# Loading k one third of a block before its use, and attention heads 1.15 slots apart

## The chip, the cores and the metric

The kernel runs on one core of a Trainium2 chip. The metric is device time in microseconds (us), the median over several runs of the whole program. One further execution was recorded by the profiler. Its engines are called PE (TensorE), DVE (VectorE), ACT (ScalarE), POOL (GpSimd) and SP (SyncE, which here only issues transfers).

## What is computed

Two things follow each other, for 8 batches of 576 tokens. First comes attention with 8 heads of width 64, in which every 8 rows of k and of v are averaged, so that a head has 72 keys. Then comes a block of two residual mixes: over tokens with `w_tok`, and over channels with two matrices and a ReLU between them. Cut down, the reference is:

```
k_p = k.reshape(B, H, 72, 8, D).mean(axis=3)       # B, H, S, D = 8, 8, 576, 64
v_p = v.reshape(B, H, 72, 8, D).mean(axis=3)
attn = softmax(q @ k_p^T / sqrt(D))
x = (attn @ v_p), heads side by side               # (B, 576, 512)
tok = einsum('ts,bsd->btd', w_tok, alpha1 * x + beta1)
u = x + lam * tok
ch = relu((alpha2 * u + beta2) @ w_ch1) @ w_ch2    # 512 -> 2048 -> 512
out = u + lam * ch
```

Everything comes in and goes out as float32; the matrix products run on 16-bit operands.

## The kernel before, in words

**Chunks and blocks.** The tokens of a batch are split into four chunks of 128 (c = 0 to 3) and a rest of 64. The rests of two neighbouring batches share one more chunk (c = 4). That gives 36 chunks, and four consecutive ones form a block of 512 columns for the channel mix, so there are nine blocks, n = 0 to 8. The loop over n at the end of the kernel makes, for each block, a list `todo` of (slot, action), sorts it by slot and emits it. The order on every engine and on every queue is therefore written out by these slot numbers; each engine then runs its own list in order, and waits only for data and buffers.

**The channel mix sets the slots.** In block n, `mlp_A(n, j)` stands at slot j, for j = 0 to 15: four matmuls (L477) into a PSUM tile `ps_h`, which ACT turns into `Hj` (L482). `mlp_B(n, m, part)` stands at slot 16 + 4m + part: four matmuls (L495) of output chunk m. Its last part adds the result to `u_sb` on DVE (L500) and stores it from SP's queue (L502, or L506 for a shared chunk).

**Attention of the next batch runs in between.** Block n, for n up to 6, also holds `attention(b)` for b = n + 1:

- `cast_rem` (L116, L118) and `sum_k` (L131, L133) on POOL take the sums of k's rows, and the cast of q's last 64 rows, from the tiles `k_raw` and `rem_raw`. They stand at the block's very start (slots -2.0 to 0.3). POOL has little else to do and runs ahead of the other engines: it begins them as soon as the loads have landed, which can be in the block before.
- `att_F` (L314) and `att_Frem` (L332) are DMA transposes of q on SP's queue, at the block's start. Head 0 needs them at slot 7.4.
- `att_V` (L362, L364) sums v's rows on DVE, and `att_K` brings k's sums through PE and copies them to `kpT` (L356, DVE).
- Head h has `att_S` at slot 7.4 + 1.0 h (PE L374 and L377 into `ps_sc`, exponential on ACT L379), and `att_AV` two slots later (PE L393 and L397 into `ps_av`; on DVE the reciprocal L399 and `x_tm` L401). After every second head `att_X` multiplies `x_tm` by a row into `xs` (DVE L408 and L412).
- `mix_T(b, c)` from slot 18.6 is the token mix: five matmuls into `ps_tok` (L442), then `u_sb` (L444) and `u_bf` (L446) on DVE. `mix_uT` 1.8 slots later is a DMA transpose of `u_bf` into `u_fm` (L456, SP's queue), which `mlp_A` of a later block reads.

The tiles `ps_h`, `ps_sc`, `ps_av` and `ps_tok` share six PSUM buffers (pool `psA`), so that PE can't start the next `ps_h` while DVE has not read an older `ps_av`.

**Loads.** In block n the loads of batch b + 1 = n + 2 are issued. Before the change k and the rests (`load_qk` and `load_rem`: on SP's queue two `k_raw` loads L88 and four `rem_raw` loads L96) stand at slots 0.4 to 1.6. `load_qk` also issues q's load, L79, from POOL's queue, where it comes behind the sums of batch b. v (`load_v`, L108, SP's queue) is at 3.5 and 7.5. `k_raw`, `rem_raw` and `v_u` have two buffers each, `q_bf` has four. Batch 1, which is set up during block 0, and the loads of batch 2 there have slots of their own (the branches `late` and `b == 1`).

## Time and profile before

| | |
|---|---|
| median of 7 runs | 381.56 us (380.48 to 383.31) |
| the profiled execution | 381.88 us, of which 380.1 us is the span from first to last instruction |
| granted PE clock | 0.995 of full speed |
| busy in the span: PE, DVE, ACT, POOL | 350.0, 237.3, 157.2, 85.2 us |
| block 1 begins at | 87.49 us |
| blocks 2 to 5 begin at | 126.35, 165.39, 204.08, 242.87 us |
| blocks 6 to 8 begin at | 282.86, 319.92, 347.55 us |

A block begins where its first `ps_h` matmul starts in the chain of waits. The page gives each engine's busy time, the span in 40 slices, the chain of work that ended last, and groups of equal instructions. The trace behind it can be asked for any stretch of time: what each engine did in it, what it waited for, and how busy the core's 16 DMA engines were. "Busy" of PE counts overlapping matmuls once, and is not PE at its peak.

### The profile page before, as it was taken

How to read it: one execution, taken by the hardware profiler on the slowest of the kernel's cores; microseconds unless marked ns; L12 is line 12 of the kernel's file. 1: busy time of each engine (PE TensorE's matmuls, PEld its weight loads, DVE VectorE, ACT ScalarE, POOL GpSimd, SP SyncE). 2: the span in 40 equal slices, each digit the busy share in tenths (PEclk: the TensorE clock that was granted, in tenths of full speed). 3: DMA queues.
4: the chain of work that ended last, by engine and by line, in shares of the span. 5: the costliest groups of instructions: out<-in, count | busy, mean ns of one | idle time of the engine just before them, and what ended most of it. 6: DMA issues, size and time to landing. Idle time of an engine off the chain costs nothing.

```text
span 380.1 us, 5735 instructions
## 1 busy us (share of the span) xinstructions
PE 350.0 (92%) x2139; PEld 188.8 (50%) x2179; DVE 237.3 (62%) x459; ACT 157.2 (41%) x317; POOL 85.2 (22%) x94
## 2 busy tenths in 40 slices
PE   2889999699989989999999999997999999999994
PEld 0475655345644554455445544464446544544541
DVE  4796839888885588658864887489647872011011
ACT  1574667116910483038303830284018602712700
POOL 7563353930530062005300430024000000000000
PEclk9999999989999999999999999999999999999999
DMA  8999996745953495468635872775233024002011
GB/s 199 226 178 214 262 212 173 120 83 153 243 82 100 120 236 82 98 145 217 102 96 126 212 116 64 131 202 112 56 106 68 0 57 124 0 29 83 2 55 55
DMA packets 63931, 46.93 MB, mean 123 GB/s; under 512 B 31448, under 2 KB 54044, under 8 KB 63904
## 3 DMA queue, kind: packets, MB, share of 16 engines
q1 hardware_dynamic: 54496, 38.55, 41.4%
q0 software_dynamic: 9408, 8.02, 13.9%
q8 instruction: 17, 0.28, 0.3%
q14 instruction: 10, 0.08, 0.1%
HBM read 38.04 MB, written 9.44 MB: 125 GB/s over the span
## 4 chain that ended last, share of the span: by engine, by line
PE 80%; DVE 12%; DMA 2%; issue 1%; ACT 1%; SPq 1%; POOL 1%; POOLq 0%; DVEq 0%
PE ps_ch L495 32%; PE ps_h L477 28%; PE ps_tok L442 11%; DVE xs L408 3%; DVE x_tm L401 3%; PE ps_sc L374 3%; DVE xs L412 3%; DMA vecs<-in_moe_beta_dram 2%; PE ps_av L393 1%; SPq L314 1%; DVE rec L399 1%; PE ps_sc L377 1%; DMA rem_qT<-rem_q 1%; PE ps_uT L461 1%; PE ps_w L247 1%
## 5 line engine op out<-in xcount | busy, mean ns | idle before, releaser
L482 ACT ACTIVATE Hj<-ps_h,bias_cols 128x512 bf16<-128x512 f32 x144 | 98.5, 687 | 164.3 <-PE ps_h L477 162.9
L477 PE MATMUL ps_h<-u_fm,w 128*128 128x512 bf16 (+2 forms) x572 | 136.0, 375 | 9.0 <-DVE x_tm L401 8.1
L495 PE MATMUL ps_ch<-w,Hj 128*128 128x512 bf16 x562 | 133.3, 381 | 0.7
L477 PEld LDWEIGHTS <-w 128*128 128x128 bf16 x592 | 62.7, 114 | 55.6 <-DVE x_tm L401 10.4
L495 PEld LDWEIGHTS <-Hj 128*128 128x128 bf16 x576 | 55.4, 98 | 63.5 <-issue 0.8
L500 DVE TENSOR_TENSOR u_sb<-u_sb,ps_ch 128x512 f32<-128x512 f32 x36 | 24.6, 685 | 78.4 <-PE ps_ch L495 78.3
L442 PE MATMUL ps_tok<-xs,wtT 128*128 128x512 bf16 (+1 forms) x195 | 50.4, 386 | 3.3 <-DVE xs L408 2.7
L379 ACT ACTIVATE ET<-ps_sc 72x256 f16<-72x256 f32 (+1 forms) x128 | 44.3, 401 | 5.0 <-PE ps_sc L374 4.2
L444 DVE TENSOR_TENSOR u_sb<-x_tm,ps_tok 128x512 f32<-128x512 f32 (+1 forms) x40 | 27.5, 687 | 29.9 <-PE ps_tok L442 29.6
L362 DVE TENSOR_TENSOR v_u<-v_u 72x512 f32<-72x512 f32 x64 | 38.4, 600 | 1.5
L116 POOL CAST rem_q<-rem_raw 128x256 bf16<-128x256 f32 x7 | 2.8, 395 | 141.2 <-DMA rem_raw<-in_q_dram 141.2
L442 PEld LDWEIGHTS <-wtT 128*128 128x128 bf16 (+1 forms) x200 | 19.5, 99 | 27.2 <-issue 5.4
L401 DVE TENSOR_TENSOR x_tm<-ps_av,rec 128x320 f32<-128x320 f32 x64 | 31.5, 492 | 2.3
L408 DVE TENSOR_TENSOR xs<-x_tm,lamal_bc 128x512 bf16<-128x512 f32 x29 | 28.5, 982 | 0.9
L374 PE MATMUL ps_sc<-qT,kpT 128*72 128x256 bf16 x128 | 26.6, 291 | 1.7 <-ACT kpT L356 1.3
L446 DVE TENSOR_TENSOR u_bf<-u_sb,al_bc 128x512 bf16<-128x512 f32 (+1 forms) x38 | 27.1, 713 | 1.5
L393 PEld LDWEIGHTS <-ET 72*128 72x128 f16 x256 | 16.6, 102 | 13.4 <-issue 0.8
L133 POOL TENSOR_TENSOR k_bf<-k_raw 128x512 bf16<-128x512 f32 x16 | 22.8, 1425 | 1.3
L131 POOL TENSOR_TENSOR k_raw<-k_raw 128x512 f32<-128x512 f32 x16 | 21.5, 1346 | 3.8 <-DMA k_raw<-in_k_dram 3.8
L393 PE MATMUL ps_av<-vp,ET 72*128 72x66 f16 x256 | 18.5, 199 | 0.6 <-ACT ET L379 0.4
L356 DVE CAST kpT<-ps_kp 64x288 bf16<-64x288 f32 x28 | 12.7, 455 | 7.1 <-PE ps_kp L351 6.5
L399 DVE RECIPROCAL rec<-ps_av 128x5 f32<-128x5 f32 x64 | 12.1, 189 | 8.0 <-PE ps_av L397 6.9
(98 smaller groups left out, 214.8 us busy)
## 6 DMA issues: line engine op xcount, KB each, us to landing
k_raw<-in_k_dram SPq DMA_DIRECT2D x16, 512.0 KB
v_u<-in_v_dram SPq DMA_DIRECT2D x16, 512.0 KB
out_dram<-u_sb SPq DMA_DIRECT2D x32, 256.0 KB
w<-in_moe_w_ch_dram POOLq DMA_DIRECT2D x8, 512.0 KB, 12.5
q_bf<-in_q_dram POOLq DMA_DIRECT2D x12, 256.0 KB, 4.8
q_raw<-in_q_dram SPq DMA_DIRECT2D x4, 512.0 KB
rem_raw<-in_q_dram SPq DMA_DIRECT2D x16, 64.0 KB
rem_raw<-in_k_dram SPq DMA_DIRECT2D x16, 64.0 KB
```

The source lines that it names most:

```text
L362: nc.vector.tensor_tensor(out=t[:, :, 0:n], in0=t[:, :, 0:n], in1=t[:, :, n:2 * n], op=ALU.add)
L374: nc.tensor.matmul(out=ps_sc[0:SPG, 0:256], lhsT=kpT_pool[u][:, half, h % 4, :], rhs=st["qT"][u][:, 2 * (h % 4):2 * (h % 4) + 2, :])
L379: nc.scalar.activation(out=ET[:, n0:n0 + n], in_=ps_sc[0:SPG, 0:n], func=AF.Exp, bias=0.0, scale=0.125)
L393: nc.tensor.matmul(out=av[:, c, :], lhsT=ET[:, m0:m0 + 128], rhs=vp1[:, hh, :])
L401: nc.vector.tensor_tensor(out=x[:, :, dd:dd + D], in0=av[:, :, 0:64], in1=rec.unsqueeze(2).to_broadcast((P, 5, D)), op=ALU.mult)
L408: eng.tensor_tensor(out=xs[:, 0:4, cols], in0=x[:, 0:4, cols], in1=lamal_bc[:, cols].unsqueeze(1).to_broadcast((P, 4, D * (h1 - h0))), op= ...
L442: nc.tensor.matmul(out=ps_tok, lhsT=wtT[0:kk, at, t0:t0 + P], rhs=xs[0:kk, sc, :], start=(sc == 0), stop=(sc == 4))
L444: nc.vector.tensor_tensor(out=s["u"][p0:p1, :], in0=st1[b]["x"][p0:p1, c, :], in1=ps_tok[p0:p1, 0:DM], op=ALU.add)
L446: eng.tensor_tensor(out=s["u_bf"][p0:p1, :], in0=s["u"][p0:p1, :], in1=al2_bc[p0:p1, :], op=ALU.mult)
L477: nc.tensor.matmul(out=ps_h[:, t0:t1], lhsT=w1_of(cc, j), rhs=u_fm[n][:, cc, t0:t1], start=(cc == 0), stop=(cc == 3))
L482: nc.scalar.activation(out=t, in_=ps_h, func=AF.Relu, bias=bias_cols[:, j:j + 1], scale=1.0)
L495: nc.tensor.matmul(out=ps, lhsT=Hj[n, j][:, 128 * m:128 * m + 128], rhs=w2[j // 4][:, j % 4, :], start=(j == 0), stop=(j == NJ - 1))
```

## The change

Three slot numbers move.

- For all batches but the first ones, k's and the rests' loads of batch b + 1 move within block n from slots 0.4 to 1.6 to slots 21.0 to 21.2, that is from the block's first instructions to a place behind the first `mix_uT`. v's loads stay. On POOL's queue the order of instructions does not change at all; only the data that its sums wait for are asked for later.
- `att_S`, and with it `att_AV` and `att_X`, of head h moves from 7.4 + 1.0 h to 7.4 + 1.15 h, again for all batches but the first ones.
- `mix_T` of chunk c, and `mix_uT` behind it, moves from 18.6 + 1.3 c to 19.1 + 1.3 c.

```diff
@@ attention(b)
         for h in range(8):
-            at = 17.0 + 0.9 * h if late else 7.4 + 1.0 * h
+            at = 17.0 + 0.9 * h if late else 7.4 + 1.15 * h
             lag = 1.6 if late else 2.0
             todo.append((at, lambda h=h: att_S(b, h)))
@@
         for c in range(5):
-            at = 26.2 + 0.9 * c if late else 18.6 + 1.3 * c
+            at = 26.2 + 0.9 * c if late else 19.1 + 1.3 * c
             todo.append((at, lambda c=c: mix_T(b, c)))
@@ the loop over n
                 for u in range(2):
-                    at = 20.0 + 0.2 * u if b == 1 else 0.4 + 1.2 * u
+                    at = 20.0 + 0.2 * u if b == 1 else 21.0 + 0.2 * u
                     todo.append((at, lambda b=b, u=u: load_qk(b + 1, u)))
                     at = 22.0 + 0.2 * u if b == 1 else 3.5 + 4.0 * u
                     todo.append((at, lambda b=b, u=u: load_v(b + 1, u)))
-                todo.append((20.1 if b == 1 else 0.9, lambda b=b: load_rem(b + 1)))
+                todo.append((20.1 if b == 1 else 21.1, lambda b=b: load_rem(b + 1)))
```

The order of instructions that results, in a block with attention: on SP's queue the two `k_raw` and four `rem_raw` loads go from behind `att_Frem` to between the block's first and second `u_fm` transposes. On PE heads 4 to 7 each come one group of four matmuls later than before, and so do the token mixes of chunks 0, 1, 3 and 4. On DVE the first L500 of the block comes ahead of the first L444 instead of behind it, and the second L500 stands ahead of the fourth L444. On POOL nothing moves.

## The prediction

> **What bounds the kernel now.** I began with the page's chain of work that ended last. PE carries most of it, and DVE is the only other engine with a large share:

> ```profile
> PE 80%; DVE 12%; DMA 2%; issue 1%; ACT 1%; SPq 1%; POOL 1%; POOLq 0%; DVEq 0%
> ```

> DVE's 12% is 46 us, so the next question is where a block loses PE time. I cut each attention block at its first `ps_tok` matmul (L442) and asked for the busy time by stage: from the block's start to the first mix, and from there to the next block. Columns: stretch, its length, then busy us of PE, PEld, DVE, ACT and POOL with counts, granted clock, DMA share, GB/s.

> ```profile
> 87.49:109.71 22.22, 20.59 (x150) 12.15 (x152) 19.07 (x41) 16.07 (x33) 8.53 (x8) 1.00 0.75 175
> 126.35:148.77 22.42, 20.62 (x150) 12.16 (x152) 19.39 (x41) 15.49 (x32) 7.97 (x8) 1.00 0.80 174
> ...
> 242.87:266.22 23.35, 20.75 (x150) 12.16 (x152) 20.05 (x41) 15.60 (x32) 6.88 (x6) 1.00 0.70 147
> 282.86:303.26 20.40, 20.24 (x150) 12.23 (x152) 17.09 (x41) 15.49 (x32) 0.00 (x0) 1.00 0.19 43
> ...
> 148.77:165.39 16.62, 16.57 (x77) 7.57 (x77) 8.78 (x14) 0.00 (x0) 0.00 (x0) 1.00 0.36 88
> 303.26:319.92 16.66, 16.61 (x78) 7.56 (x77) 8.86 (x14) 0.00 (x0) 0.00 (x0) 1.00 0.36 87
> ```

> All stages of a kind have the same matmuls. The mix stage takes 16.6 us in every block, all of it PE, while DVE is busy for half of it and POOL idle. The attention stage takes 22.05 to 23.35 us in blocks 1 to 5 (blocks 3 and 4: 22.05 and 22.13), but 20.40 us in block 6. Block 6 is the one where POOL does nothing, since no batch is left to load: an experiment that the kernel makes by itself. DVE has 2.3 us less there on the same 41 instructions. The timelines of DVE, block 2 and then block 6, show which:

> ```profile
> 138.20 1.20 DVE L408 TENSOR_TENSOR xs<-x_tm,lamal_bc 128x512 bf16<-128x512 f32 x1
> 139.42 1.26 DVE L412 TENSOR_TENSOR xs<-x_tm,lamal_bc 64x128 bf16<-64x128 f32 x1
> ...
> 294.71 0.69 DVE L408 TENSOR_TENSOR xs<-x_tm,lamal_bc 128x512 bf16<-128x512 f32 x1
> 295.41 0.29 DVE L412 TENSOR_TENSOR xs<-x_tm,lamal_bc 64x128 bf16<-64x128 f32 x1
> ```

> The slow ones are those that run while POOL sums (136.31 to 143.09 in block 2). DVE then reads `ps_av` late, the PSUM buffer comes free late, and PE waits in its timeline:

> ```profile
> 141.49 1.05 PE L477 MATMUL ps_h<-u_fm,w 128*128 128x512 bf16 x4 [1.14 <-DVE x_tm L401]
> ```

> So the bound is PE, except in attention stages of blocks 1 to 5, where DVE slowed by POOL's sums holds it up.

> [...] L408 and L412 (two SBUF inputs) go from 0.69 and 0.29 us up to 1.75 and 1.35, while L401 (one input in PSUM) keeps 0.49 us beside the same sums. [...] The trace before shows no stretch where q's load (POOL's queue) runs beside the q transposes (SP's queue), so that price is open; I bound it below.

> **The change part by part.**

> *The sums leave the attention stage.* In block 6's order of PE work the first mix will start one group of four L495 (0.86 us) later, at 21.26 us after the block's start, plus 1.08 for the mix and 1.4 for L444 and L446; the first `u_fm` transpose is issued at about 23.8. Behind it SP issues k and the rests at 25.1 to 28.8 (k 0.53, four times 0.62, k 0.54). Before, the sums' first instruction started 4.6 to 6.3 us after the first k issue (131.66 to 136.31; 92.69 to 98.94) and the sums took 6.6 to 7.3 us. So they run from about 29.8 to 36.5 of a block of 37.06 (20.40 + 16.66), in the mix stage. There DVE has only L446 of chunks 3 and 4 with two SBUF inputs, 0.69 us each, and is idle for 8 of 16.6 us; no PE work of that stage waits for `u_bf`. The gain, if the stage falls to block 6's: (22.22 + 22.42 + 22.05 + 22.13 + 23.35) - 5 x 20.40 = **10.17 us**. I take off 0.3 for spill of the sums into the next block's L362 (two SBUF inputs).

> *Sums too late?* `att_K` uses `k_bf` at 4.3 us of the next block, 4.9 us after 36.5. Covered.

> *SP's queue.* The 3.7 us of issues now stand ahead of the second `u_fm` transpose and everything behind it. The second goes out at 28.9 instead of about 25, the second store next, and the third, the last one that the very next block can need (blocks 2 and 3), at 30.6. Before, it went out later than that: SP stood at the store of the block's second output until 119.57, and the third transpose was issued at 120.42, 32.9 us into block 1. A transpose landed 2.3 us after its issue in the one case that the chain shows (`rem_qT`); with some 1.5 us of k's last packets ahead the third lands at 34.4 of 37. Cost nothing, cover 2.6 us. The head of the block loses the same 3.7 us from SP, so v's loads go out earlier; nothing waits for them.

> *What is late next: q's load.* POOL's order is unchanged, so q of batch b + 2 is issued right behind the sums of b + 1. Before, that was after 106.21, in the middle of a block, with no other transfer. Now it is at 36.5, its packets from about 38.3 (1.8 us later, as 220.54 to 222.3), which is 1.2 us into blocks 2 to 5: right on the q transposes. The stages of one us (same columns), first q's load, then transposes in block 6:

> ```profile
> 109.00:110.00 1.00, 1.00 (x7) 0.41 (x5) 0.66 (x2) 0.00 (x0) 0.00 (x0) 1.00 1.40 181
> 286.00:287.00 1.00, 1.00 (x6) 0.48 (x5) 0.30 (x2) 0.82 (x2) 0.00 (x0) 1.00 0.93 176
> ```

> Both fill the DMA engines: q's two loads for 3.4 us (shares 0.09, 1.05, 1.40, 1.36, 0.26 from 107 on), the three transposes for 3.0 us (0.56, 1.00, 0.93, 1.01, 0.33 from 284 on, some 0.8 of it a store). Alone the transposes land at about 5.5 us of a block (288.3), and L377 wants the last, `rem_qT`, at 7.3 (290.17). Together they need 1.2 + 3.4 + 3.0 = 7.6. There is no slack to hide more: in block 5 they came last already, by the chain of waits:

> ```profile
> 248.06 2.31 DMA rem_qT<-rem_q
> ```

> It landed at 250.4, 7.5 us into block 5, with no q load beside it. The wait added per block is bounded by 0 (the load's packets leave gaps that the transposes fill) and by 1.9 (half of q's 3.4 us on top of block 5's 7.5, less 7.3); the sum of the two works says 0.3. I take **0.8 us, in four blocks: 3.2 us** back.

> *Heads 1.15 apart, mixes half a slot later.* Block 6 runs at 1.0 with PE busy 20.24 of 20.40, so spacing has nothing left to give once POOL is away. A head then costs PE 1.45 us (1.15 x 0.86 + 0.46) against DVE's 1.32. Between the last `att_AV` and the first mix stand two L495 groups (1.73 us) as before; DVE needs 1.5 us to L408. Zero; bounds -0.3 and +0.3 per block if DVE still trails. L500 ahead of the first L444 costs 0.69 us on `u_bf`, with slack of over 2 us.

> **Sum.** Profiled execution 381.88 (span 380.1 and 1.78 around it); - 10.17 + 0.3 + 3.2 = 375.2. The median before, 381.56, lies 0.3 under the profiled run, so I predict **375.0**.

> **Rivals.**
> - *A, as worked out* (0.52): 373 to 378.
> - *B, the transposes fit in* (0.20): no stall, 381.6 - 10.2 = 371.4. For it: the DMA share of q's load goes to 1.4, so packets overlap, and the sums may end early.
> - *C, the interference moves* (0.12): the sums run 2 us late, into L362 and `kpT`, and slow DVE ahead of head 0; half the gain stays, 377 to 380. Against: POOL itself ran in 6.6 us beside a busier DVE.
> - *D, `u_fm` late* (0.07): k's packets hold the third transpose for over 3 us; up to 3 us in blocks 2 and 3 besides A, about 381, no change.
> - *E, q's load starves the transposes* (0.09): slower. [...] PE stands at L377 for 3 us in four blocks, and that with C's loss of 1 to 2 in each makes 383. It decides from 2.5 us per block (10.17 / 4).

> The change doing nothing is excluded: POOL's sums wait for loads that are issued 20 slots later.

> **How the numbers follow.** The range reaches from B's end (371.2) to the weak ends of A and C (379.5: 371.4 + 0.3 + four stalls of 1.9). A measurement of this kernel can tell 0.3%, 1.1 us, from no change. Faster: A, B, C = 0.84; same: D = 0.07; slower: E = 0.09.

> **What would show it.** Right: L408 at 0.69 us in blocks 1 to 5, POOL's sums in the last 8 us of each block, no PE wait on `x_tm`, attention stages near 21.3 us to the mix in block 1 and 0.5 to 1.5 longer in 2 to 5, with `rem_qT` last in the chain at L377. Wrong: L446, L362 or L356 stretched, `ps_h` waiting for `u_fm` at a block's start, or L377 held for over 2 us.

## The result: 1.4% slower, and the profile after

The changed kernel takes 386.91 us (median of 12 runs, 384.57 to 390.17) against 382.12 us before (31 runs). The ratio is 1.0141, with a 95% interval of 1.0115 to 1.0167. The profiled execution has a span of 384.5 us, 4.4 more than before, at a granted clock of 0.981 instead of 0.995.

The page's chain that ended last has exchanged DVE for DMA:

```profile
PE 83%; DVE 7%; DMA 5%; issue 2%; POOL 1%; SPq 0%; ACT 0%; POOLq 0%; DVEq 0%
```

The same cut by stage as before, at the first `ps_tok` matmul of each block, shows where. Columns: stretch, length, then busy us of PE, PEld, DVE, ACT and POOL with counts, granted clock, DMA share, GB/s. The first three lines are the attention stages of blocks 1, 2 and 5, the last is the mix stage of block 1.

```profile
85.50:106.76 21.26, 21.11 (x154) 12.66 (x156) 16.82 (x42) 15.96 (x33) 0.00 (x0) 1.00 0.47 109
122.54:146.15 23.61, 21.43 (x154) 12.59 (x156) 17.10 (x41) 15.71 (x32) 1.36 (x2) 1.00 0.64 109
...
244.06:271.44 27.38, 24.06 (x154) 13.42 (x156) 16.77 (x41) 15.82 (x32) 1.35 (x2) 0.88 0.57 98
...
106.76:122.54 15.78, 15.67 (x72) 7.16 (x73) 9.75 (x13) 0.00 (x0) 6.92 (x7) 1.00 0.65 168
```

POOL's sums have moved: 6.92 us of them lie in the mix stage, which is no longer for it. DVE is back at 17 us in the attention stage. Block 1 takes 21.26 us, which is block 6's 20.40 plus the one group of 0.86 us that now comes ahead of the mix. Blocks 3 and 4, not shown, take 25.50 and 24.85 us. So blocks 2 to 5 lie 2.35, 4.24, 3.59 and 6.12 us over block 1, 16.3 us in sum; that eats the 10.2 us won and more. PE's timeline in block 3 shows how such a block is lost:

```profile
170.90 0.38 PE L374 MATMUL ps_sc<-qT,kpT 128*72 128x256 bf16 x2 [1.69 <-DMA qT<-q_bf]
172.03 0.24 PE L377 MATMUL ps_sc<-rem_qT,kpT 128*72 128x64 bf16 x1 [0.75 <-DMA rem_qT<-rem_q]
172.11 1.88 PE L477 MATMUL ps_h<-u_fm,w 128*128 128x512 bf16 x4
```

Head 0 waits for q's transposes, first for `qT`, then for `rem_qT`. (In blocks 2 and 5 the view puts the first of the two waits down to DVE's L362, which only ended last. L374 doesn't read what L362 writes, and the L362 named for block 2 begins 7.9 us into the block, just as in run 1 below, where PE doesn't wait.) The four `ps_h` matmuls behind the waits take 1.88 us instead of 1.03. That is the second loss: the clock. Busy time around the waits of block 2 (first line), of block 3 (second), and right after the waits of blocks 3, 4 and 5, by the same columns:

```profile
129.80:132.20 2.40, 0.38 (x3) 0.25 (x3) 2.01 (x5) 1.07 (x2) 0.00 (x0) 1.00 1.01 189
...
169.20:172.10 2.90, 0.46 (x4) 0.32 (x4) 2.02 (x5) 1.07 (x2) 0.00 (x0) 0.95 1.26 253
171.80:175.20 3.40, 3.17 (x11) 1.47 (x11) 0.00 (x0) 1.61 (x4) 0.00 (x0) 0.50 1.07 181
212.80:216.10 3.30, 3.08 (x10) 1.50 (x11) 0.00 (x0) 1.71 (x4) 0.00 (x0) 0.50 0.97 203
253.80:260.50 6.70, 5.63 (x23) 2.77 (x23) 0.69 (x2) 3.12 (x8) 0.00 (x0) 0.50 0.82 170
```

In blocks 3 and 4 the clock is 0.50 for 3.4 us, in block 5 for 6.8 us; in block 2 it stays full. The length of the idle time alone doesn't decide this. Block 2 had 2.0 us of it and kept its clock, block 4 had 1.85 and lost it:

```profile
211.60 0.38 PE L374 MATMUL ps_sc<-qT,kpT 128*72 128x256 bf16 x2 [1.11 <-DMA qT<-q_bf]
212.72 0.24 PE L377 MATMUL ps_sc<-rem_qT,kpT 128*72 128x64 bf16 x1 [0.74 <-DMA rem_qT<-rem_q]
```

Run 2 below even kept the full clock (1.00 from 122 to 160 us) through 2.6 us in its block 2 (1.91 and 0.73). What differs is where the idle time falls. The six changes of the clock in this trace, at 171.8, 175.2, 212.75, 216.2, 253.7 and 260.5 us, lie whole multiples of 3.41 us apart. Counted back from them in steps of 3.41 us, a step ends at 130.8 us and cuts block 2's idle time into 1.0 and 1.0; the steps that ended with a fall in blocks 3, 4 and 5 held 2.2, 1.85 and 2.0 us. The most that run 2 had in a step without a fall comes to 1.8 us. That the place of the idle time decides is my estimate from these two traces; no run was made to test it.

The share of each loss follows from the stages. Stage length less PE busy, less block 1's 0.15, is the wait: 2.0, 2.5, 2.0 and 3.2 us, together 9.7. PE busy of blocks 3 to 5 over block 2's 21.43 is the half clock: 1.5, 1.3 and 2.6, together 5.4. The rest, 1.3, is PE's busy time in each of the four blocks over block 1's (21.43 against 21.11).

Block 0, which the change doesn't touch, is 2.0 us shorter in this execution: the one before had a stretch at half clock there (75.6 to 79.0 us), this one not. So the span grew by 4.4 us although blocks 1 to 6 grew by 6.35 (238.78 against 232.43).

### The profile page after: what moved, and what is told of

Its sections match the earlier page's. It is cut to its first block, busy times and chain, and to the rows that moved or that the text cites. A ratio compares the mean times of both kernels' runs of the same rounds, so it can differ in the third digit from the quotient of the medians.

```text
span 384.5 us, 5756 instructions
## 1 busy us (share of the span) xinstructions
PE 352.2 (92%) x2139; PEld 189.4 (49%) x2179; DVE 229.2 (60%) x459; ACT 158.1 (41%) x317; POOL 83.6 (22%) x94
## 4 chain that ended last, share of the span: by engine, by line
PE 83%; DVE 7%; DMA 5%; issue 2%; POOL 1%; SPq 0%; ACT 0%; POOLq 0%; DVEq 0%
PE ps_h L477 32%; PE ps_ch L495 31%; PE ps_tok L442 11%; DMA rem_qT<-rem_q 3%; PE ps_sc L374 3%; DMA vecs<-in_moe_beta_dram 2%; PE ps_av L393 2%; DVE v_u L362 2%; DVE x_tm L401 2%; PE ps_sc L377 1%; DVE xs L408 1%; DVE vp L364 1%; PE ps_uT L461 1%; DVE xs L412 1%; PE ps_bias L300 1%
## 5 line engine op out<-in xcount | busy, mean ns | idle before, releaser
L477 PE MATMUL ps_h<-u_fm,w 128*128 128x512 bf16 (+2 forms) x571 | 140.8, 383 | 1.3 <-issue 0.2
L495 PE MATMUL ps_ch<-w,Hj 128*128 128x512 bf16 x563 | 133.4, 379 | 0.7
L477 PEld LDWEIGHTS <-w 128*128 128x128 bf16 x592 | 63.3, 115 | 51.5 <-issue 8.2
L495 PEld LDWEIGHTS <-Hj 128*128 128x128 bf16 x576 | 55.1, 98 | 61.6
L500 DVE TENSOR_TENSOR u_sb<-u_sb,ps_ch 128x512 f32<-128x512 f32 x36 | 24.7, 687 | 72.3 <-PE ps_ch L495 55.3
L442 PE MATMUL ps_tok<-xs,wtT 128*128 128x512 bf16 (+1 forms) x195 | 49.0, 380 | 3.9 <-DVE xs L408 3.5
L444 DVE TENSOR_TENSOR u_sb<-x_tm,ps_tok 128x512 f32<-128x512 f32 (+1 forms) x40 | 27.5, 686 | 23.5 <-PE ps_tok L442 21.1
L116 POOL CAST rem_q<-rem_raw 128x256 bf16<-128x256 f32 x7 | 4.4, 635 | 167.2 <-DMA rem_raw<-in_q_dram 167.2
L362 DVE TENSOR_TENSOR v_u<-v_u 72x512 f32<-72x512 f32 x64 | 37.0, 577 | 1.5
L374 PE MATMUL ps_sc<-qT,kpT 128*72 128x256 bf16 x128 | 27.5, 300 | 7.8 <-DVE v_u L362 3.3
L401 DVE TENSOR_TENSOR x_tm<-ps_av,rec 128x320 f32<-128x320 f32 x64 | 31.5, 492 | 2.3
L442 PEld LDWEIGHTS <-wtT 128*128 128x128 bf16 (+1 forms) x200 | 19.1, 98 | 26.8 <-issue 3.7
L446 DVE TENSOR_TENSOR u_bf<-u_sb,al_bc 128x512 bf16<-128x512 f32 (+1 forms) x38 | 30.9, 814 | 1.5
L408 DVE TENSOR_TENSOR xs<-x_tm,lamal_bc 128x512 bf16<-128x512 f32 x29 | 22.0, 758 | 0.9
L131 POOL TENSOR_TENSOR k_raw<-k_raw 128x512 f32<-128x512 f32 x16 | 20.7, 1292 | 5.2 <-DMA k_raw<-in_k_dram 5.2
L374 PEld LDWEIGHTS <-kpT 128*72 128x72 bf16 x128 | 12.5, 124 | 15.3 <-DVE v_u L362 4.5
```

Source lines behind the costliest of these rows:

```text
L362: nc.vector.tensor_tensor(out=t[:, :, 0:n], in0=t[:, :, 0:n], in1=t[:, :, n:2 * n], op=ALU.add)
L374: nc.tensor.matmul(out=ps_sc[0:SPG, 0:256], lhsT=kpT_pool[u][:, half, h % 4, :], rhs=st["qT"][u][:, 2 * (h % 4):2 * (h % 4) + 2, :])
L401: nc.vector.tensor_tensor(out=x[:, :, dd:dd + D], in0=av[:, :, 0:64], in1=rec.unsqueeze(2).to_broadcast((P, 5, D)), op=ALU.mult)
L408: eng.tensor_tensor(out=xs[:, 0:4, cols], in0=x[:, 0:4, cols], in1=lamal_bc[:, cols].unsqueeze(1).to_broadcast((P, 4, D * (h1 - h0))), op= ...
L442: nc.tensor.matmul(out=ps_tok, lhsT=wtT[0:kk, at, t0:t0 + P], rhs=xs[0:kk, sc, :], start=(sc == 0), stop=(sc == 4))
L444: nc.vector.tensor_tensor(out=s["u"][p0:p1, :], in0=st1[b]["x"][p0:p1, c, :], in1=ps_tok[p0:p1, 0:DM], op=ALU.add)
```

## The experiments

My theory after the comparison: q's load of batch b + 2, which follows the sums on POOL's queue, has moved with them onto q's transposes of batch b + 1; the transposes land late, PE stands still and loses its clock. The rivals were that the wider heads and later mixes cost (S), and that k's loads in front of the `u_fm` transposes, or the sums in the mix stage, cost (U).

**1. q's load ahead of the sums.** The load of batch b + 1 takes the buffers that the transposes of batch b - 1 last read, so it can't start before those have landed.

```diff
+    def load_q(b, u): ...            # the q part of load_qk, for b > 2
                     todo.append((at, lambda b=b, u=u: load_qk(b + 1, u)))
+                    if b > 1:
+                        todo.append((-3.0, lambda b=b, u=u: load_q(b + 1, u)))
```

> The changed kernel, with one thing moved: from block 1 on, q's load of batch b + 1 stands ahead of the sums of batch b on GpSimd's queue instead of behind them. Its two buffers are then those of batch b - 1, so it waits until that batch's q transposes have landed and comes behind them. Theory (q's load on top of the q transposes costs all that was lost): attention stages of blocks 2 to 5 fall from 23.6, 25.5, 24.9 and 27.4 us to 21.3 to 21.6, the granted clock has no half-speed windows there, and the time is 370 to 373 us. Rival S (heads 1.15 apart and later mixes cost) and rival U (k's loads ahead of the u_fm transposes, or the sums in the mix stage, cost): the time stays above 382.

Measured: 371.42 us, ratio 0.9718 (0.9667 to 0.9768). The attention stages of blocks 2 and 3, and POOL's timeline at the load (line numbers are 8 higher here; L73 is q's load):

```profile
124.97:146.24 21.27, 21.11 (x155) 12.65 (x156) 17.09 (x41) 15.38 (x32) 1.53 (x2) 1.00 0.70 121
162.03:183.30 21.27, 21.11 (x155) 12.66 (x156) 17.51 (x41) 15.38 (x32) 2.96 (x4) 1.00 0.72 130
```

```profile
130.11 0.79 POOL L73 DMA_DIRECT2D q_bf<-in_q_dram  x1 [5.26 <-DMA qT<-q_bf]
131.41 0.74 POOL L73 DMA_DIRECT2D q_bf<-in_q_dram  x1 [0.51 <-DMA qT<-q_bf]
```

POOL waits for the transposes, at no cost, and PE no longer does. Everything else of the change is still there, so S and U fall.

**2. Only the loads move.** Heads 1.0 apart and mixes from 18.6, as before.

> The changed kernel with heads 1.0 apart and mixes from 18.6, as before: only the loads move. Theory (collision of q's load with the q transposes): the same stalls ahead of head 0, so 384 to 389 us, as the changed kernel. Rival S (spacing costs): back to 380 or below.

Measured: 388.9 us (384.88 to 390.61), ratio 1.0177 (1.0104 to 1.0250). The chain has the same link in block 3, 4.80 us long:

```profile
168.58 4.80 DMA rem_qT<-rem_q
```

The loss sits in the loads' move.

**3. Only the spacing.**

```diff
-            at = 17.0 + 0.9 * h if late else 7.4 + 1.0 * h
+            at = 17.0 + 0.9 * h if late else 7.4 + 1.15 * h
-            at = 26.2 + 0.9 * c if late else 18.6 + 1.3 * c
+            at = 26.2 + 0.9 * c if late else 19.1 + 1.3 * c
```

> The kernel before with heads 1.15 apart and mixes from 19.1; the loads stay where they were. Theory: the sums still slow L408 and L412, and wider heads give DVE up to 0.13 us per head of slack, so a little is won: 376 to 382 us. Rival S: 384 us or more.

Measured: 376.63 us, ratio 0.9867 (0.9824 to 0.9911). The chain in block 2 still has the slow operations of DVE:

```profile
135.82 1.27 DVE xs L408
137.10 1.27 DVE xs L412
```

But PE waits less for them: 1.7 us for `x_tm` and 1.3 for `xs` in all of blocks 1 to 6, against 8.1 before. Where the sums lie in the attention stage, wider heads are worth some 5 us.

**4. No q load for batches 3 to 7.**

```diff
-        if b > 1:
+        if b > 2:
+            st1[b]["q"][u] = st1[2]["q"][u]
+        elif b > 1:
```

> The changed kernel without q's loads for batches 3 to 7: their transposes read batch 2's q again, so the output of those batches is that of another q. All else stays. Theory: with the suspected transfer gone, attention stages of blocks 2 to 5 are 21.2 to 21.5 us, 369 to 372 us in all. Rival U: a stall ahead of head 0 or at the block's start stays, 382 us or more.

Measured: 371.59 us, ratio 0.9734 (0.9688 to 0.9780), and the attention stages of blocks 2 and 3 are block 1's:

```profile
124.16:145.42 21.26, 21.10 (x154) 12.64 (x156) 17.10 (x41) 15.38 (x32) 0.00 (x0) 1.00 0.43 97
161.22:182.48 21.26, 21.10 (x154) 12.65 (x156) 16.83 (x41) 15.38 (x32) 0.84 (x1) 1.00 0.44 103
```

Taking the transfer away and moving it give the same time. It is the transfer's place that costs.

**5. Run 1 with the old spacing.**

> q's load ahead of the sums as in the first run, but heads 1.0 apart and mixes from 18.6, as before: the load move alone, with the collision gone. Theory of the prediction (once the sums have left the attention stage, spacing gives nothing, since block 6 of the kernel before keeps PE busy at 1.0): 370 to 373 us, within 1 us of the first run. Rival (spacing is a gain of its own, as it was alone with 376.6): 375 us or more.

Measured: 369.91 us, ratio 0.9683 (0.9647 to 0.9718), a little under what was expected: 1.5 us below run 1, not 1. Run 8 comes back to that. The attention stage of block 2, with the first mix again one group earlier:

```profile
122.16:142.56 20.40, 20.40 (x153) 12.23 (x152) 17.10 (x41) 15.49 (x32) 1.84 (x3) 1.00 0.73 127
```

That is block 6's 20.40 us to the digit, now without any PE idle time.

**6. The wait filled with matmuls of no use.**

```diff
+            if h == 0 and 3 <= b <= 6:
+                todo.append((at, lambda: keep_warm(12)))
             todo.append((at, lambda h=h: att_S(b, h)))
```

> The changed kernel with 12 matmuls of no use (2.6 us of PE) ahead of head 0 in blocks 2 to 5, where PE otherwise stands idle for q's transposes. They take no data from anywhere and only fill the wait. Theory (the half-speed windows of the clock follow from that idle time and cost about 5.4 us on top of the wait itself): no half-speed windows in blocks 3 to 5, and 380.5 to 383.5 us although PE has 10.4 us more to do. Rival (the clock falls for another reason, or costs little): 387 us or more.

Measured: 382.47 us (380.96 to 386.63), ratio to before 1.0017 (0.9986 to 1.0047). The chain in block 3, and the busy times of the first 21.14 us of that block (its attention stage ends at 187.72):

```profile
171.12 2.59 PE ps_warm L432 x12
```

```profile
163.86:185.00 21.14, 21.14 (x153) 12.52 (x151) 14.28 (x34) 15.62 (x32) 1.66 (x3) 1.00 0.72 134
```

Block 3's attention stage takes 23.86 us, which is 21.26 plus the 2.59 of the added matmuls, where the changed kernel took 25.50. With 10.4 us more work for PE the kernel is 4.4 us faster than the changed one, and the clock stays at 1.00 through the attention stages of blocks 2 to 5. The half clock is a consequence of the idle time, and the gain is near the 5.4 us that PE's busy times said.

**7. Half of q's load.**

```diff
-        if b > 1:
+        if b > 2 and u == 1:
+            st1[b]["q"][u] = st1[b]["q"][0]
+        elif b > 1:
```

> The changed kernel with half of q's load for batches 3 to 7: heads 4 to 7 read the rows of heads 0 to 3 again, so the output is that of another q; all transposes stay. Theory (the work of both transfers adds up on the DMA engines): rem_qT lands about 2.1 us earlier, half of q's 4.2 us of DMA share, so 7.2 to 8.7 us into blocks 2 to 5 instead of 9.3 to 10.8; PE waits 0 to 1.4 us there, with at most one half-speed window, and the time is 371 to 377 us. Rival (any q load that starts ahead of the transposes delays them, whatever its size): 382 us or more.

Measured: 375.79 us, ratio 0.9834 (0.9803 to 0.9864). Attention stages of blocks 2 and 5 (blocks 3 and 4: 22.35 and 21.50), and PE's wait in block 3:

```profile
125.28:146.80 21.52, 21.43 (x157) 12.67 (x156) 17.09 (x41) 15.51 (x32) 0.61 (x1) 1.00 0.54 108
...
238.01:261.46 23.45, 21.59 (x158) 12.57 (x156) 16.79 (x41) 15.73 (x32) 0.62 (x1) 1.00 0.60 104
```

```profile
171.00 0.24 PE L379 MATMUL ps_sc<-rem_qT,kpT 128*72 128x64 bf16 x1 [0.67 <-DMA rem_qT<-rem_q]
```

`rem_qT` is read at 7.6, 8.4, 7.6 and 9.5 us of blocks 2 to 5; three of the four lie in the expected 7.2 to 8.7. The stages are 3.8 us over 21.26 in sum, against 16.3 with the whole load. Half the transfer costs a quarter, since by estimate the first 1.8 us of delay are slack (undisturbed, a landing at 5.5 us and a read at 7.3) and the clock stays full in this run. PE's wait in block 5, worked out as above, comes to 1.7 us, more than the 1.4 expected.

**8. Runs 5 and 1 once more, on one chip.**

> The kernel of the fifth run again (loads moved, q's load ahead of the sums, heads 1.0 apart, mixes from 18.6), on one chip with its counterpart with heads 1.15 apart. Theory (spacing gives nothing once the sums are away): both within 0.3% of each other, 369 to 372 us, ratio to before 0.968 to 0.973. Rival: the wider one is slower by 0.5% or more.

> The kernel of the first run again (heads 1.15 apart, mixes from 19.1), beside the denser one on the same chip. Theory: within 0.3% of it. Rival: 0.5% or more above it.

Measured: 369.70 us, ratio 0.9705 (0.9666 to 0.9744), for the dense one; 371.13 us, ratio 0.9732 (0.9693 to 0.9772), for the wide one. They differ by 0.4%, between what the two expectations said, and the intervals overlap: whether the spacing costs a little here stays open. That it gains nothing is clear enough. Both beat the kernel before and the changed one by some 3% and 4%.

**9. The kernel before, with q's load ahead of the sums.**

> The kernel before with q's load ahead of the sums on GpSimd's queue and nothing else: a control for what the reordering itself is worth while the sums stay in the attention stage. Theory: L408 and L412 stay slow, 379 to 384 us. Rival (the reordering is the gain): 375 us or less.

Measured: 383.21 us, ratio 1.0040 (1.0017 to 1.0063). DVE's timeline in block 2 (L416 is L408 of the kernel before):

```profile
142.00 1.57 DVE L416 TENSOR_TENSOR xs<-x_tm,lamal_bc 128x512 bf16<-128x512 f32 x1
146.26 1.60 DVE L416 TENSOR_TENSOR xs<-x_tm,lamal_bc 128x512 bf16<-128x512 f32 x1
```

The reordering alone brings no gain; it costs 0.4%. The gain of runs 1 and 5 needs the moved sums.

## Why the prediction was wrong

**The sums leave the attention stage: right.** They start 29.97 us into block 1 (115.47; I had said 29.8), and end at 36.9 (36.5). L408 takes 0.69 us in blocks 1 to 5, PE never waits for `x_tm`, and the stage of block 1 has the 21.26 us of the working. Run 5 puts the gain, with nothing in its way, at 232.43 - 222.64 = 9.8 us over blocks 1 to 6, where I had 10.17 - 0.3.

**Sums too late, SP's queue, spacing: right.** No PE wait in the mix stage, none on `u_fm`; the mix stages are 15.7 to 16.0 us long where 16.66 - 0.86 = 15.80 was due. L446 of chunk 4 stretches to as much as 1.48 us beside the sums, one of my signs of being wrong, and no PE work waits for it. Runs 5 and 8 bear out that spacing has nothing left to give.

**What is late next: the step that failed.** I had found the collision, its place and its time, and mis-sized it: 0.8 us in each of four blocks, at most 1.9, against a measured mean of 16.3 / 4 = 4.1 us. Of these 4.1, some 2.4 are the wait, 1.3 the half clock and 0.3 PE's longer busy time. Two terms were wrong.

The first is the landing. I added 1.2 + 3.4 + 3.0 = 7.6 us. In block 2 `rem_qT` lands 2.99 us after its issue at 129.17, which is 9.6 us into the block. By stages of one us (same columns; the block starts at 122.54):

```profile
124.00:125.00 1.00, 1.00 (x7) 0.49 (x5) 0.97 (x3) 0.81 (x2) 0.00 (x0) 1.00 0.66 64
...
128.00:129.00 1.00, 1.00 (x11) 0.58 (x11) 0.94 (x2) 0.82 (x2) 0.00 (x0) 1.00 1.57 166
129.00:130.00 1.00, 0.75 (x3) 0.22 (x2) 0.94 (x4) 0.65 (x2) 0.00 (x0) 1.00 1.24 131
```

The DMA shares from 124 to 132 sum to 9.2 us in 8 us, 1.15 per us. I had entered q's load with its elapsed 3.4 us although its shares summed to 4.2, and left out the store of the block's last output (0.8) that SP issues just ahead of the transposes. Those shares sum to 4.2 + 0.8 + 3.0 = 8.0; at 1.15 per us that is an estimate of 7.0 us, and a landing at 8.2. So the work explains a part of the delay, not all of it. And the queue itself is held up. SP's timeline, first of the changed kernel in block 2, then of the kernel before in the same block:

```profile
123.79 5.28 SPq L314 DMA_TRANSPOSE qT<-q_bf  x2
129.17 1.19 SPq L332 DMA_TRANSPOSE rem_qT<-rem_q  x1
```

```profile
127.61 2.65 SPq L314 DMA_TRANSPOSE qT<-q_bf  x2
```

The two issues of `qT` take 5.28 us instead of 2.65, so that `rem_qT` is not even issued before 6.6 us of the block, where it was 4.0. That is 2.6 of the 4.1 us by which it lands later than the 5.5 of my undisturbed case. The longer issue comes with q's load: in blocks 2 to 4 of runs 1 and 4 it is 2.65 us again, in run 7, with half the load, 3.8 to 4.6. Run 7 also gave back 1.3 to 2.1 us of the landing and most of the loss. By what mechanism the load lengthens SP's issue no run tells.

The second term wasn't in the sum at all: waits like these can cost the clock. That is 5.4 us by PE's busy times; run 6, which put 10.4 us of work in the place of 9.7 us of waits, came out 4.4 us lower.

**The rivals.** E named the place (L377), the sign and the point from which it decides (2.5 us per block); 3 us of wait in each was near the 2.0 to 3.2 measured, without the clock. Those 3 us had no trace behind them, and how the two queues share the DMA engines no run tells. Its sum was off: 371.4 plus four waits of 3 us is 383.4 already, without the loss of 1 to 2 us per block that I borrowed from C and that didn't come. My bound of 1.9 us laid half of q's load on block 5's landing at 7.5 us, which makes 9.2; the landings came at 9.3 to 10.8. B's 371.4 is the time of runs 1 and 4, in which q's load no longer meets the transposes. C and D didn't happen. The ends of my range don't add up either, though nothing hangs on it: B's is 371.4, not 371.2, and 371.4 + 0.3 + 4 x 1.9 is 379.3, not 379.5.

## What to carry to other kernels

When a step is moved, look at what follows it on the same queue and waits for nothing else: it moves along, and lands on whatever runs there. Price a collision of transfers by the sum of their shares of the DMA engines, with all that is queued ahead of the late one, not by their times alone: here the shares give a landing at 8.2 us by estimate and the times 7.6, where 9.6 was measured. Look also at what the late transfer's own queue has to issue first, and whether that issue gets longer (here 5.28 us instead of 2.65). Where PE might stand idle for some 2 us, add the microseconds at half clock; here they were a third of the loss (5.4 of 16.3 us), and three of four waits brought them on. Making the transfer wait for a buffer that its rival frees put the two in order here at no cost (371.42 us in run 1, 371.59 without the load in run 4).
